# A fused attention and two-MLP kernel: the middle third of kv summed by TensorE, a shorter weight conversion, values transposed from the keys, weights loaded earlier

## The chip, the cores and the metric

The kernel runs on one core of one Trainium2 chip. The metric is device time in microseconds (us) of one execution, the median of the runs. The engines of the core are TensorE (PE in the profile, its weight loads PEld), VectorE (DVE), ScalarE (ACT), GpSimd (POOL) and SyncE (SP), whose queue issues every transfer here.

## The reference

Three stages follow one another on 12,288 tokens of width 128. The attention has one head; its keys and its values are the same array, the kv image averaged over 4 by 4 patches and multiplied by `w_sr`, so there are 768 of them.

```python
kv_pool = kv.reshape(B, H//4, 4, W//4, 4, C).mean(axis=(2, 4))   # 768 rows of 128
k = v = kv_pool.reshape(B, -1, C) @ w_sr
a = softmax(q @ k.T / sqrt(C));  x = a @ v                        # 12288 x 128
h = x @ w_in1;  g = max(h, 0) + alpha * min(h, 0);  y = g @ w_out1   # 128 -> 2048 -> 128
h = y @ w_in2;  g = h * sigmoid(1.702 * h);         z = g @ w_out2   # 128 -> 2048 -> 128
```

`q`, `kv`, `w_sr` are float32. The four MLP matrices arrive as float64 and go to the chip as pairs of 32-bit words.

## The kernel before, in words

Every product of the main part is made of three float16 products: both operands are split into a high part and a low remainder (`parts` L313, `mm3` L101), and high·high, high·low and low·high are added in PSUM. The high part is a ScalarE copy, the low part a subtraction on VectorE or GpSimd.

**Blocks and steps.** The tokens go in 24 blocks of 512. A step `t` of the main loop (`step` L547, loop L597) takes one of 16 slices of 128 hidden units through each of four layers, each layer for another block: layer 1 at `t`, layer 2 four steps later, layer 3 31 steps later, layer 4 36 steps later (L38). So t = 0 is the first layer-1 product, t = 16 the first of block 1, and layer 3 starts at t = 31. The attention of a block (scores `a_s`, exponentials `a_e`, high and low part of the weights `a_h` and `a_l` with a DMA transpose each, products with the values `a_v`) is laid over the steps before its layer 1 by the tables `ATT_START`, `ATT_S`, `ATT_V` (L40 to L42). The loop begins at t = -18 with block 0's attention.

**Before the loop.** kv lies in memory as 128 channels by 12,288 values, the 16 values of a patch side by side. It comes in twelve pieces of 512 KB, five buffers of tile `kv`; VectorE sums each group of 16 (L475) into `kvt`. After each third of the 768 keys, `thirds` (L446) forms the keys with `w_sr` in float32 (`keys`, L452: channels by keys), the same values a second time with the keys as rows (`low`, L459: the `pv` tiles), and takes the largest key (L461). Between the pieces the list `todo` (L468) puts the conversion of the first weight matrix. `v_scale` (L491) takes one scale from the three maxima and splits the keys into `k_hi` and `k_lo`; the split of block 0's queries follows (L595); `v_split` (L507), at t = -14, splits the `pv` tiles into `v_hi` and `v_lo`.

**Weights.** A float64 matrix comes in two pieces of 1 MB into tile `raw` (four buffers, `load_w` L138). `stats` (L148) takes the largest absolute value from the high words (two reductions, L152, and a row of small operations). Three steps then make float32 of the two words of a number: `conv1` scales the high word on ScalarE (L181), shifts and masks it (L182, recorded at L110) and puts the sign in (L185); `conv2` masks the exponent out (L191, recorded at L108), multiplies it by 16 bits of the low word (L195) and adds that on GpSimd (L197); `conv3` makes the float16 high part on ScalarE (L204) and the low part on GpSimd (L205). `conv2` also issues the load four pieces further on. `STATS` and `PREP` (L45, L46) give the steps at which w2, w3 and w4 are taken.

The order on each engine's queue is fixed at build time by a list scheduler. The order in which the program writes things is their priority; work whose inputs the scheduler holds ready may move ahead of what waits.

Of the kernel before, what the change touches and what calls it, by code (L numbers as in the profile page):

```python
# [38 lines left out]

ATT_START = [-18, -9] + [KF * j - 25 for j in range(2, NB)]  # L40
ATT_S = [(0, 2, 2, 6), (0, 4, 11, 13)] + [(0, 4, 7, 12)] * (NB - 2)
ATT_V = [tuple(range(10, 16)), tuple(range(17, 23))] + [(17, 18, 19, 21, 22, 22)] * (NB - 2)  # L42
# [10 lines left out]
def attn_moe_kernel(ctx: ExitStack, tc: tile.TileContext, q, kv, w_sr, w_in1, w_out1, alpha, w_in2, w_out2, out):  # L53
    nc = tc.nc
    const = ctx.enter_context(tc.tile_pool(name="const", bufs=1))
    raw_p = ctx.enter_context(tc.tile_pool(name="raw", bufs=4))
    cv_p = ctx.enter_context(tc.tile_pool(name="cv", bufs=2))
# [80 lines left out]
    def load_w(key, c):  # L138
        t = raw_p.tile([P, CW, 2], I32, tag="raw", name=f"raw_{key}{c}")
        src = srcs[key].bitcast(I32)  # L140
        if key in ("w1", "w3"):
            nc.sync.dma_start(out=t.rearrange("p f t -> p (f t)"), in_=src[:, 2 * c * CW:2 * (c + 1) * CW])
        else:
            nc.sync.dma_start(out=t.rearrange("p (k d) t -> p k (d t)", k=KC),
                              in_=src[c * CW:(c + 1) * CW, :].rearrange("(k p) d -> p k d", p=P))
        raw[key, c] = t
# [29 lines left out]
    def conv1(i):  # L176
        key, c = order[i]
        d = cv[i] = {}
        d["g"] = cv_p.tile([P, CW], I32, tag="g", name="g")

        nc.scalar.activation(d["g"].bitcast(F32), raw[key, c][:, :, 1].bitcast(F32), AF.Copy, scale=gsc[key])  # L181
        ts(d["g"], d["g"], 3, ALU.logical_shift_left, 0x7FFFFFFF, ALU.bitwise_and)  # L182

        d["a"] = cv_p.tile([P, CW], I32, tag="a", name="a")
        nc.vector.scalar_tensor_tensor(out=d["a"], in0=raw[key, c][:, :, 1], scalar=-0x80000000, in1=d["g"],  # L185
                                       op0=ALU.bitwise_and, op1=ALU.bitwise_or)

    def conv2(i):
        key, c = order[i]
        d = cv[i]  # L190
        ts(d["g"], d["a"], -0x800000, ALU.bitwise_and)  # L191

        u = raw[key, c].rearrange("p f t -> p (f t)").bitcast(U16).rearrange("p (f t) -> p f t", t=4)[:, :, 1]
        d["w"] = cv_p.tile([P, CW], F32, tag="w", name="w")
        nc.vector.scalar_tensor_tensor(out=d["w"], in0=u, scalar=2.0 ** -36, in1=d["g"].bitcast(F32),  # L195
                                       op0=ALU.mult, op1=ALU.mult)
        nc.gpsimd.tensor_tensor(out=d["w"], in0=d["a"].bitcast(F32), in1=d["w"], op=ALU.add)  # L197
        if i + 4 < len(order):
            load_w(*order[i + 4])
# [16 lines left out]
    def q_split(j):  # L216
        src = q_t.pop(j)
        qh[j] = at_p.tile([P, TB], F16, tag="qh", name="qh")
        ql[j] = at_p.tile([P, TB], F16, tag="ql", name="ql")
        c, p = scale_of(qsc[j], ps_x.tile([P, TB], F32, tag="x", name="qt"), None, "q")  # L220
        u = sm_p.tile([P, 1], F32, tag="qu", name="qu", bufs=4)
        qsc[j] = u

        def f():
            ts(u, p, kq, ALU.mult)
            parts(qh[j], ql[j], src, c)

        late.append(f)

# [208 lines left out]
    TK = NKEY // 3  # L438
    pvs = []
    vm = kv_p.tile([P, 3], F32, name="vm", bufs=1)  # L440
    todo = []

    kp2 = ps_s2.tile([P, 2, 512], F32, tag="s", name="kp2")
    pks = [kp2[:, 0, :], kp2[:, 1, :]]

    def thirds(i):  # L446
        tk = slice(i * TK, (i + 1) * TK)

        def keys():
            if i == 2:  # L450
                pks.append(ps_y.tile([P, TB], F32, tag="y", name="pk"))
            mm(out=pks[i][:, 0:TK], lhsT=wsr, rhs=kvt[:, tk], start=True, stop=True)  # L452

        def low():
            if i != 1:
                pvs.append(((ps_x if i else ps_y).tile([P, TB], F32, tag="x" if i else "y", name="pv"),
                            slice(2 * i, min(2 * i + 4, KT))))
            for k in (2 * i, 2 * i + 1):
                mm(out=pvs[-1][0][:, (k % 4) * C:(k % 4 + 1) * C], lhsT=kvt[:, k * P:(k + 1) * P], rhs=wsr,  # L459
                   start=True, stop=True)  # L460
            nc.vector.tensor_reduce(out=vm[:, i:i + 1], in_=pks[i][:, 0:TK], axis=AX.X, op=ALU.max,  # L461
                                    apply_absolute_value=True)

        c = 8 * i + 8 - NC2
        todo.append((c + 4, keys))
        todo.append((c + 6, low))

    for n, f in enumerate((lambda: stats("w1"), lambda: conv1(0), lambda: conv2(0), lambda: (conv3(0), conv1(1)),  # L468
                           lambda: conv2(1), lambda: conv3(1))):
        todo.append((4 + 2 * n, f))  # L470
    for c in range(0, NCH, NC2):
        t = kv_p.tile([P, NC2 * TB], F32, tag="kv", name="kv", bufs=5)
        nc.sync.dma_start(out=t, in_=kv[:, c * TB:(c + NC2) * TB])
        i, c8 = divmod(c, 8)
        nc.vector.tensor_reduce(out=kvt[:, c * 32:(c + NC2) * 32], in_=t.rearrange("p (k r) -> p k r", r=R * R),  # L475
                                axis=AX.X, op=ALU.add)
        if c == 6:
            load_q(0)
        if c8 == 8 - NC2:
            thirds(i)  # L480
        while todo and (min(x[0] for x in todo) <= c or c == NCH - NC2):
            x = min(todo, key=lambda x: x[0])
            todo.remove(x)
            x[1]()
        if c == 6:
            a_q(0)
    for c in range(NCW):
        load_w("w2", c)
    load_q(1)

    def v_scale():  # L491
# [11 lines left out]
        for i, t in enumerate(pks):
            tk = slice(i * TK, (i + 1) * TK)
            parts(k_hi[:, tk], k_lo[:, tk], t[:, 0:TK], vsc.bitcast(F32))

    def v_split():  # L507
        for t, k in pvs:
            src = t[:, 0:(k.stop - k.start) * C]
            hi, lo = (x[:, k, :].rearrange("p k d -> p (k d)") for x in (v_hi, v_lo))  # L510
            parts(hi, lo, src, vsc.bitcast(F32))

# [30 lines left out]
    def flush():  # L543
        while late:
            late.pop(0)()

    def step(t):  # L547
# [24 lines left out]
        for j, p in pieces:  # L572
            for n, p0 in enumerate(ATT_S[j]):
                if p == p0:
                    a_s(j, n)
            for k, p0 in enumerate(ATT_V[j]):
                if p == p0:
                    a_v(j, k)
            if p == -6 and j > 0:
                a_q(j)  # L580
            if p == -4 and j > 0:
                q_split(j)
                if j + 1 < NB:
                    load_q(j + 1)
# [63 lines left out]
```

## Time and profile before

| what | value |
|---|---|
| median of 3 runs | 1317.21 us (1317.12 to 1317.59) |
| the profiled execution, its own time | 1318.12 us |
| its span, first to last record | 1316.0 us |
| its mean granted TensorE clock | 0.982 |
| busy in the span: PE, DVE, ACT, POOL | 1226.0, 1053.4, 1108.5, 800.2 us |

The span of one execution is read by engine and by stage. The stages used below are cut at events: 38.24 us, the last key maximum has been taken; 48.47, the first score product starts; 85.42, the first layer-1 product (t = 0); 143.39, the first layer-1 product of block 1 (t = 16); 176.74, the first activation of layer 3 (t = 32). A busy TensorE is not one at its peak, since matmuls overlap. Idle time in brackets or after a bar is that of the engine just before an instruction, with what ended it.

### The profile page before, as it was taken

What the parts mean: (1) busy time and instruction counts of PE and PEld (TensorE: products, weight loads), DVE (VectorE), ACT (ScalarE), POOL (GpSimd) and SP (SyncE); (2) the same over time, 40 slices, a digit from 0 to 9 for tenths busy, and PEclk for the clock granted to TensorE, in tenths of its full rate; (3) what the DMA queues carried; (4) which work ended last, traced back from release to release, by engine and by line L of the source; (5) the groups of instructions that cost most, each with busy time, mean ns of one, the idle gap of its engine ahead of it and who ended that gap; (6) DMA issues with size and microseconds to landing.
All of it is one profiled execution on the core that took longest, in us unless ns stands there. A gap on an engine that the chain in (4) does not pass through costs nothing.

```text
span 1316.0 us, 17933 instructions
## 1 busy us (share of the span) xinstructions
PE 1226.0 (93%) x5712; PEld 560.1 (43%) x5712; DVE 1053.4 (80%) x1901; ACT 1108.5 (84%) x1966; POOL 800.2 (61%) x678
## 2 busy tenths in 40 slices
PE   1466699999999999999999999999999999999998
PEld 1122244444444444444444444444444444444443
DVE  7889789787887887878878878878878878877666
ACT  1455698998988988988988988988989989988998
POOL 1146743756756756756666666666666656657774
PEclk9877899999999999999999999999999999999999
DMA  9341221321211211212212212112112211210000
GB/s 355 98 120 24 45 51 32 52 51 26 54 44 33 53 41 37 53 33 44 53 32 45 47 37 47 40 37 53 41 37 46 47 37 33 45 36 21 9 9 17
DMA packets 167359, 66.26 MB, mean 50 GB/s; under 512 B 154848, under 2 KB 159072, under 8 KB 166752
## 3 DMA queue, kind: packets, MB, share of 16 engines
q1 hardware_dynamic: 167264, 65.11, 21.6%
q8 instruction: 45, 0.74, 0.2%
q14 instruction: 50, 0.41, 0.1%
HBM read 21.05 MB, written 6.29 MB: 21 GB/s over the span
## 4 chain that ended last, share of the span: by engine, by line
PE 54%; ACT 15%; DVE 14%; issue 5%; DMA 0%; POOLq 0%; ACTq 0%; DVEq 0%
PE h L102 8%; PE h L104 7%; PE h L103 7%; PE y L103 7%; PE y L104 7%; PE y L102 7%; DVE g L341 4%; ACT g L340 3%; ACT g L395 3%; ACT s L256 3%; DVE g L396 2%; PE xacc L103 2%; PE xacc L104 2%; ACT g1h L348 2%; PE xacc L102 2%
## 5 line engine op out<-in xcount | busy, mean ns | idle before, releaser
L349 POOL TENSOR_TENSOR g1l<-g,g1h 128x512 f16<-128x512 f32 x384 | 453.8, 1187 | 321.9 <-ACT g1h L348 310.1
L405 POOL TENSOR_TENSOR g2l<-g,g2h 128x512 f16<-128x512 f32 x272 | 314.8, 1158 | 120.7 <-ACT g2h L403 110.9
L395 ACT ACTIVATE g<-h,yu 128x512 f32<-128x512 f32 x384 | 269.2, 701 | 104.3 <-PE h L104 101.2
L396 DVE SCALAR_TENSOR_TENSOR g<-g,h 128x512 f32<-128x512 f32 x384 | 262.5, 684 | 110.7 <-ACT g L395 105.0
L341 DVE SCALAR_TENSOR_TENSOR g<-g,oma,h 128x512 f32<-128x512 f32 x384 | 285.1, 743 | 58.5 <-ACT g L340 52.4
L340 ACT ACTIVATE g<-h 128x512 f32<-128x512 f32 x384 | 235.8, 614 | 22.6 <-PE h L104 11.4
L348 ACT CAST g1h<-g 128x512 f16<-128x512 f32 x384 | 244.1, 637 | 8.5 <-DVE g L341 8.3
L403 ACT CAST g2h<-g 128x512 f16<-128x512 f32 x384 | 243.6, 634 | 3.3 <-PE y L104 1.2
L103 PE MATMUL y<-g1l,w2h 128*128 128x512 f16 x384 | 146.6, 382 | 14.7 <-POOL g1l L349 14.7
L102 PE MATMUL h<-xh,w1h 128*128 128x512 f16 x384 | 145.9, 382 | 5.4 <-DVE g L341 4.6
L102 PE MATMUL y<-g1h,w2h 128*128 128x512 f16 x384 | 146.2, 381 | 3.4 <-ACT g1h L348 3.4
L102 PE MATMUL h<-yh,w3h 128*128 128x512 f16 x384 | 145.2, 378 | 4.0 <-DVE g L341 1.0
L103 PE MATMUL h<-xl,w1h 128*128 128x512 f16 x384 | 146.7, 382 | 1.3
L104 PE MATMUL h<-xh,w1l 128*128 128x512 f16 x384 | 146.7, 382 | 0.0
L104 PE MATMUL y<-g1h,w2l 128*128 128x512 f16 x384 | 146.7, 382 | 0.0
L103 PE MATMUL y<-g2l,w4h 128*128 128x512 f16 x384 | 145.5, 379 | 0.5 <-POOL g2l L405 0.5
L102 PE MATMUL y<-g2h,w4h 128*128 128x512 f16 x384 | 145.5, 379 | 0.0
L104 PE MATMUL y<-g2h,w4l 128*128 128x512 f16 x384 | 145.5, 379 | 0.0
L104 PE MATMUL h<-yh,w3l 128*128 128x512 f16 x384 | 145.4, 379 | 0.0
L103 PE MATMUL h<-yl,w3h 128*128 128x512 f16 x384 | 145.3, 378 | 0.0
L246 DVE TENSOR_REDUCE nm<-s 128x1 f32<-128x768 f32 x96 | 91.5, 953 | 11.9 <-PE s L241 8.3
L405 DVE TENSOR_TENSOR g2l<-g,g2h 128x512 f16<-128x512 f32 x112 | 90.0, 804 | 9.7 <-ACT g2h L403 9.7
(228 smaller groups left out, 1686.0 us busy)
## 6 DMA issues: line engine op xcount, KB each, us to landing
kv<-in_kv SPq DMA_DIRECT2D x12, 512.0 KB, 8.4
q<-in_q SPq DMA_DIRECT2D x24, 256.0 KB, 2.6
out<-ob SPq DMA_DIRECT2D x24, 256.0 KB, 2.0
raw_w<-in_moe_w_in SPq DMA_DIRECT2D x4, 1024.0 KB, 8.5
raw_w<-in_moe_w_out SPq DMA_DIRECT2D x4, 1024.0 KB, 7.0
eh<-ah SPq DMA_TRANSPOSE x96, 2.8
wsr<-in_w_sr SPq DMA_DIRECT2D x1, 64.0 KB, 2.3
al<-in_moe_alpha SPq DMA_DIRECT2D x1, 8.0 KB, 1.7
```

Of the source, the lines that this page charges most:

```text
L102: mm(out=o, lhsT=wh, rhs=xh, start=start, stop=False)
L103: mm(out=o, lhsT=wh, rhs=xl, start=False, stop=False)
L104: mm(out=o, lhsT=wl, rhs=xh, start=False, stop=stop)
L246: nc.vector.tensor_reduce(out=nm, in_=s[:, :, 0:HALF], axis=AX.XY, op=ALU.max, negate=True)
L340: nc.scalar.activation(g, h, AF.Relu, scale=-1.0)
L341: nc.vector.scalar_tensor_tensor(out=g, in0=g, scalar=oma[:, m:m + 1], in1=h, op0=ALU.mult, op1=ALU.add)
L348: nc.scalar.copy(hi, g)
L349: nc.gpsimd.tensor_tensor(out=lo, in0=g, in1=hi, op=ALU.subtract)
L395: nc.scalar.activation(g, h, AF.Tanh, scale=ysc[j][:, 0:1])
L396: nc.vector.scalar_tensor_tensor(out=g, in0=g, scalar=1.0, in1=h, op0=ALU.add, op1=ALU.mult)
L403: nc.scalar.copy(hi, g)
L405: e.tensor_tensor(out=lo, in0=g, in1=hi, op=ALU.subtract)
```

## The change

- The middle third of kv is laid out on the host so that one value of all 256 patches is contiguous. TensorE multiplies those 16 slices by `w_sr` and adds the results in PSUM; VectorE sums the first and the last third as before.
- The conversion loses two VectorE masks, the multiply and the GpSimd addition. The top three bits of the low word are shifted and OR-ed in instead.
- `v_hi` and `v_lo` are two DMA transposes of `k_hi` and `k_lo`; the `pv` products, their tiles and `v_split` go.
- `raw` has six buffers. SP issues block 0's queries, both pieces of w1, kv, then w2, block 1's queries and w3, all before the key scale; w4 at t = -8. The two `w_out` matrices are rearranged on the host, so each load is 8 KB in a row per partition.
- Block 0's queries are split before kv. Their factor with the key scale is formed by a function of its own (`q_scale`), for every block.
- Block 1's attention starts at t = -5 in place of -9, and the weight steps move by one or two.

```diff
-ATT_START = [-18, -9] + [KF * j - 25 for j in range(2, NB)]
-ATT_S = [(0, 2, 2, 6), (0, 4, 11, 13)] + [(0, 4, 7, 12)] * (NB - 2)
-ATT_V = [tuple(range(10, 16)), tuple(range(17, 23))] + ...
-V_SPLIT = -14
-STATS = {"w2": -10, "w3": 2, "w4": 6}
-PREP = [(-9, -8, -7), (-7, -6, -5), (3, 4, 5), (6, 7, 8), (9, 10, 11), (12, 13, 14)]
+ATT_START = [-18, -5] + [KF * j - 25 for j in range(2, NB)]
+ATT_S = [(0, 2, 2, 6), (0, 3, 6, 9)] + [(0, 4, 7, 12)] * (NB - 2)
+ATT_V = [tuple(range(10, 16)), tuple(range(12, 18))] + ...
+KV_FREE = -11
+W4_LOAD = -8
+STATS = {"w2": -9, "w3": 1, "w4": 8}
+PREP = [(-8, -7, -6), (-7, -6, -5), (2, 3, 4), (5, 6, 7), (10, 11, 12), (13, 14, 15)]
...
-    raw_p = ctx.enter_context(tc.tile_pool(name="raw", bufs=4))
+    raw_p = ctx.enter_context(tc.tile_pool(name="raw", bufs=6))
...
     def conv1(i):
-        ts(d["g"], d["g"], 3, ALU.logical_shift_left, 0x7FFFFFFF, ALU.bitwise_and)
-        nc.vector.scalar_tensor_tensor(out=d["a"], in0=raw[key, c][:, :, 1], scalar=-0x80000000, in1=d["g"], ...)
+        ts(g, g, 3, ALU.logical_shift_left)
     def conv2(i):
-        ts(d["g"], d["a"], -0x800000, ALU.bitwise_and)
-        nc.vector.scalar_tensor_tensor(out=d["w"], in0=u, scalar=2.0 ** -36, in1=d["g"].bitcast(F32), ...)
-        nc.gpsimd.tensor_tensor(out=d["w"], in0=d["a"].bitcast(F32), in1=d["w"], op=ALU.add)
-        if i + 4 < len(order):
-            load_w(*order[i + 4])
+        nc.vector.scalar_tensor_tensor(out=g, in0=raw[key, c][:, :, 1], scalar=-0x80000000, in1=g,
+                                       op0=ALU.bitwise_and, op1=ALU.bitwise_or)
+        nc.vector.scalar_tensor_tensor(out=g, in0=raw[key, c][:, :, 0], scalar=29, in1=g,
+                                       op0=ALU.logical_shift_right, op1=ALU.bitwise_or)
...
+    def thirds(i):
+        for n in range(4):
+            c = 8 * i + 2 * n
+            t = kv_p.tile([P, NC2 * TB], F32, tag="kv", name="kv", bufs=5)
+            nc.sync.dma_start(out=t, in_=kv[:, c * TB:(c + NC2) * TB])
+            if i == 1:
+                for r in range(4):
+                    mm(out=pks[i], lhsT=wsr, rhs=t[:, r * TK:(r + 1) * TK], start=n + r == 0, stop=n + r == 6)
+            else:
+                nc.vector.tensor_reduce(out=kvt[:, c * 32:(c + NC2) * 32], ...)
+        if i != 1:
+            mm(out=pks[i], lhsT=wsr, rhs=kvt[:, tk], start=True, stop=True)
+    a_q(0); stats("w1"); q_split(0); flush()
+    thirds(0); conv1(0); conv2(0); conv3(0)
+    thirds(1); k_max(0); conv1(1); conv2(1); conv3(1)
+    thirds(2)
     for c in range(NCW):
         load_w("w2", c)
     load_q(1)
+    for c in range(NCW):
+        load_w("w3", c)
+    k_max(1); k_max(2)
...
     def v_scale():
+        for v, k in ((v_hi, k_hi), (v_lo, k_lo)):
+            nc.sync.dma_start_transpose(out=v, in_=k)
...
     v_scale()
-    q_split(0)
-    flush()
+    q_scale(0)
+    x_bound()
```

(In the new program each of the calls joined by `;` above stands on a line of its own.)

## Rows read from the trace of the kernel before

**Rows 1.** Windows by stage: us, each engine's busy time (instructions), granted clock, DMA.
```profile
0.00:38.24 38.24, 7.59 (x19) 5.15 (x20) 28.14 (x42) 5.70 (x5) 10.11 (x10) 1.00 0.90 344
38.24:48.47 10.23, 0.88 (x4) 0.24 (x4) 9.99 (x37) 3.02 (x7) 0.00 (x0) 1.00 0.01 3
48.47:85.42 36.95, 20.46 (x67) 8.53 (x67) 33.19 (x69) 18.59 (x27) 9.97 (x4) 0.69 0.57 135
85.42:143.39 57.97, 38.75 (x137) 15.28 (x136) 49.40 (x83) 32.89 (x52) 38.32 (x23) 0.78 0.20 32
143.39:176.74 33.35, 28.70 (x136) 13.03 (x136) 25.27 (x52) 26.17 (x47) 19.45 (x17) 1.00 0.26 54
...
400.00:1200.00 800.00, 796.67 (x3787) 366.34 (x3786) 643.73 (x1162) 718.40 (x1296) 516.25 (x449) 1.00 0.20 42
```

**Rows 2.** Groups by shape, DVE, 0 to 38.2: count | busy us, mean ns.
```profile
L108 DVE TENSOR_SCALAR g<-a 128x1024 int32<-128x1024 int32 x2 | 2.6, 1304 | 0.0
```

**Rows 3.** Windows, 10 to 20 us, columns as in the first group.
```profile
10.00:20.00 10.00, 2.70 (x7) 1.67 (x6) 9.17 (x22) 2.32 (x2) 0.00 (x0) 1.00 1.02 418
```

**Rows 4.** Timeline of SP's queue: start us, us.
```profile
13.94 0.43 SPq L142 DMA_DIRECT2D raw_w<-in_moe_w_in  x1
15.08 12.40 SPq L473 DMA_DIRECT2D kv<-in_kv  x5
```

**Rows 5.** Timeline of TensorE, first float32 key product and the next.
```profile
16.79 1.22 PE L452 MATMUL kp<-kvt,wsr 128*128 128x256 f32 x2 [2.40 <-DVE b_w L108]
17.80 0.63 PE L459 MATMUL pv<-wsr,kvt 128*128 128x128 f32 x2
```

**Rows 6.** DMA issues: count, KB, median us from issue to landing.
```profile
kv<-in_kv SPq DMA_DIRECT2D x12, 512.0 KB, 8.4
...
eh<-ah SPq DMA_TRANSPOSE x96, 2.8
```

**Rows 7.** Timeline, last three kv sums on VectorE.
```profile
33.01 3.46 DVE L475 TENSOR_REDUCE kvt<-kv 128x64 f32<-128x1024 f32 x3
```

**Rows 8.** Groups by shape, DVE, 38.24 to 48.47.
```profile
L152 DVE TENSOR_REDUCE wm<-raw_w 128x1 f32<-128x1024 f32 x4 | 4.8, 1209 | 0.0
```

**Rows 9.** Timeline, low parts of the values.
```profile
45.09 1.13 DVE L315 SCALAR_TENSOR_TENSOR v_lo<-pv,vsc,v_hi 128x512 f16<-128x512 f32 x2
```

**Rows 10.** Groups by shape, DVE, 48.47 to 85.42.
```profile
L246 DVE TENSOR_REDUCE nm<-s 128x1 f32<-128x768 f32 x7 | 6.7, 950 | 2.3 <-PE s L241 2.3
...
L185 DVE SCALAR_TENSOR_TENSOR a<-raw_w,g 128x1024 int32<-128x1024 int32 x2 | 2.4, 1216 | 0.0
L152 DVE TENSOR_REDUCE wm<-raw_w 128x1 f32<-128x1024 f32 x2 | 2.4, 1202 | 0.0
...
L108 DVE TENSOR_SCALAR g<-a 128x1024 int32<-128x1024 int32 x2 | 1.4, 681 | 0.0
...
L281 DVE SCALAR_TENSOR_TENSOR al__323<-e,r,ah 128x768 f16<-128x768 f32 x1 | 1.0, 1007 | 0.0
```

**Rows 11.** Groups by shape, DVE, 85.42 to 143.39.
```profile
L185 DVE SCALAR_TENSOR_TENSOR a<-raw_w,g 128x1024 int32<-128x1024 int32 x4 | 6.8, 1692 | 0.0
L195 DVE SCALAR_TENSOR_TENSOR w<-raw_w,g 128x1024 f32<-128x1024 uint16 x4 | 6.7, 1668 | 0.0
L108 DVE TENSOR_SCALAR g<-a 128x1024 int32<-128x1024 int32 x4 | 6.2, 1538 | 0.0
L110 DVE TENSOR_SCALAR g<-g 128x1024 int32<-128x1024 int32 x4 | 6.1, 1514 | 0.0
```

**Rows 12.** Groups by shape, POOL, 85.42 to 143.39.
```profile
L197 POOL TENSOR_TENSOR w<-a,w 128x1024 f32<-128x1024 f32 x4 | 9.4, 2352 | 3.0 <-DVE w L195 1.9 <-DVE we L108 1.2
```

**Rows 13.** Timeline: one GpSimd and one VectorE instruction that overlap.
```profile
106.78 2.83 POOL L205 TENSOR_TENSOR w3l<-w,w3h 128x1024 f16<-128x1024 f32 x1
...
107.56 3.13 DVE L185 SCALAR_TENSOR_TENSOR a<-raw_w,g 128x1024 int32<-128x1024 int32 x1
```

**Rows 14.** Waits, 85.42 to 143.39: us in total, times, longest.
```profile
PE y L103 <- POOL g1l L349: 11.7, 8, 4.1
```

More of the change, by code (lines that the diff above doesn't have):

```diff
@@ L139, in load_w @@
         t = raw_p.tile([P, CW, 2], I32, tag="raw", name=f"raw_{key}{c}")
[L140 to L145, printed above, removed]
+        nc.sync.dma_start(out=t.rearrange("p f t -> p (f t)"), in_=srcs[key].bitcast(I32)[:, 2 * c * CW:2 * (c + 1) * CW])
         raw[key, c] = t
@@ L203, in conv3, with flush @@
         cs = slice(c * CW, (c + 1) * CW)
-        nc.scalar.copy(wh[key][:, cs], cv[i]["w"])
-        nc.gpsimd.tensor_tensor(out=wl[key][:, cs], in0=cv[i]["w"], in1=wh[key][:, cs], op=ALU.subtract)
+        g = cv[i].bitcast(F32)
+        nc.scalar.copy(wh[key][:, cs], g)
+        nc.gpsimd.tensor_tensor(out=wl[key][:, cs], in0=g, in1=wh[key][:, cs], op=ALU.subtract)
     late = []
+    def flush():
+        while late:
+            late.pop(0)()
     qh, ql, qsc, xacc, eh, el, xh, xl, xsc = ({} for _ in range(9))
@@ L220, in q_split, with q_scale @@
         c, p = scale_of(qsc[j], ps_x.tile([P, TB], F32, tag="x", name="qt"), None, "q")
+        qsc[j] = p
+        late.append(lambda: parts(qh[j], ql[j], src, c))
+    def q_scale(j):
         u = sm_p.tile([P, 1], F32, tag="qu", name="qu", bufs=4)
+        ts(u, qsc[j], kq, ALU.mult)
         qsc[j] = u
[L224 to L228, printed above, removed]
     st = {}
@@ L425, in attn_moe_kernel @@
     kv_ctx = ExitStack()
-    kv_p = kv_ctx.enter_context(tc.tile_pool(name="kvp", bufs=3))
-    kvt = kv_p.tile([P, NKEY], F32, name="kvt", bufs=1)
+    kv_p = kv_ctx.enter_context(tc.tile_pool(name="kvp", bufs=1))
+    kvt = kv_p.tile([P, NKEY], F32, name="kvt")
+    vm = kv_p.tile([P, 3], F32, name="vm")
     make_identity(nc, ident)
@@ L432, in attn_moe_kernel @@
     nc.sync.dma_start(out=wsr, in_=w_sr)
+    load_q(0)
     for c in range(NCW):
@@ L438, in attn_moe_kernel @@
     TK = NKEY // 3
-    pvs = []
-    vm = kv_p.tile([P, 3], F32, name="vm", bufs=1)
-    todo = []
     kp2 = ps_s2.tile([P, 2, 512], F32, tag="s", name="kp2")
-    pks = [kp2[:, 0, :], kp2[:, 1, :]]
+    pks = [kp2[:, 0, 0:TK], kp2[:, 1, 0:TK], ps_y.tile([P, TB], F32, tag="y", name="pk")[:, 0:TK]]
     def thirds(i):
         tk = slice(i * TK, (i + 1) * TK)
[L449 to L486, printed above, removed]
+        for n in range(4):
[6 more added lines that the diff above has]
+            else:
+                nc.vector.tensor_reduce(out=kvt[:, c * 32:(c + NC2) * 32], in_=t.rearrange("p (k r) -> p k r", r=R * R),
+                                        axis=AX.X, op=ALU.add)
@@ L487, in attn_moe_kernel, with k_max @@
+        if i != 1:
+            mm(out=pks[i], lhsT=wsr, rhs=kvt[:, tk], start=True, stop=True)
+    def k_max(i):
+        nc.vector.tensor_reduce(out=vm[:, i:i + 1], in_=pks[i], axis=AX.X, op=ALU.max, apply_absolute_value=True)
+    a_q(0)
+    stats("w1")
+    q_split(0)
+    flush()
+    thirds(0)
+    conv1(0)
+    conv2(0)
+    conv3(0)
+    thirds(1)
+    k_max(0)
+    conv1(1)
+    conv2(1)
+    conv3(1)
+    thirds(2)
     for c in range(NCW):
@@ L489, in attn_moe_kernel @@
     load_q(1)
+    for c in range(NCW):
+        load_w("w3", c)
+    k_max(1)
+    k_max(2)
     def v_scale():
@@ L499, in v_scale @@
         ts(vsc, vun, -1.0, ALU.mult, float(268 << 23), ALU.add)
+        for i, t in enumerate(pks):
+            tk = slice(i * TK, (i + 1) * TK)
+            parts(k_hi[:, tk], k_lo[:, tk], t, vsc.bitcast(F32))
+        for v, k in ((v_hi, k_hi), (v_lo, k_lo)):
+            nc.sync.dma_start_transpose(out=v, in_=k)
         ts(kq, vun.bitcast(F32), SCALE * 2.0 ** -32, ALU.mult)
         ts(vun, vun, float(-33 << 23), ALU.add)
[L503 to L511, printed above, removed]
     def x_bound():
@@ L541, in at @@
         return (j, m) if 0 <= j < NB else None
-    def flush():
-        while late:
-            late.pop(0)()
     def step(t):
@@ L582, in step @@
                 q_split(j)
+                late.append(lambda j=j: q_scale(j))
                 if j + 1 < NB:
@@ L601, in attn_moe_kernel @@
         step(t)
-        if t == V_SPLIT:
-            v_split()
-            x_bound()
+        if t == W4_LOAD:
+            for c in range(NCW):
+                load_w("w4", c)
+        if t == KV_FREE:
             kv_ctx.close()
@@ L631 @@
             a = a.view(np.int64)
+            if name.endswith("_w_out"):
+                a = np.ascontiguousarray(a.reshape(KF, P, C).transpose(1, 0, 2).reshape(P, DFF))
         if name == "q":
@@ L635 @@
         if name == "kv":
-            a = np.ascontiguousarray(a[0].reshape(HH // R, R, WW // R, R, C).transpose(4, 0, 2, 1, 3).reshape(C, NTOK))
+            a = a[0].reshape(HH // R, R, WW // R, R, C).transpose(4, 0, 2, 1, 3).reshape(C, 3, NKEY // 3, R * R)
+            a = np.concatenate([a[:, 0].reshape(C, -1), a[:, 1].transpose(0, 2, 1).reshape(C, -1),
+                                a[:, 2].reshape(C, -1)], axis=1)
         if name == "moe_alpha":
```

16 lines of the change are left out of this document (4 added, 12 removed).

## Prediction

> **What bounds the kernel now.** I read the windows first, cut at the events named above. Over the long middle TensorE is busy 796.67 of 800 us at a granted clock of 1.00 [rows 1]: there it sets the pace, and the change touches none of its products. What can move is the start. In the first four stages, 143.39 us together, TensorE is busy 67.7 us, part of it at a granted clock of 0.69 and 0.78 [rows 1]. From t = 16 on it is busy 28.70 of 33.35 us, and soon after always. So the end moves by about as much as t = 16 moves, and the question is what paces the four stages.
>
> In all four it is VectorE: 28.14 of 38.24, 9.99 of 10.23, 33.19 of 36.95, 49.40 of 57.97 us busy [rows 1], the first stage with 10.1 us idle. Not all of that is work. In stage four the sixteen VectorE instructions of the conversion take 6.8 + 6.7 + 6.2 + 6.1 = 25.8 us [rows 11]; undisturbed, at 1.216 for one with two tensors and 0.681 for one with one [rows 10], they would take 4 x 3.79 = 15.2. The timeline shows why: an instruction that began at 107.56 while GpSimd worked from 106.78 to 109.61 took 3.13 us, about what was left of GpSimd's plus its own 1.2 [rows 13]. GpSimd's four additions are 9.4 us of this stage [rows 12], and TensorE waits 11.7 us for the low parts that GpSimd makes [rows 14].
>
> **The change, stage by stage.**
>
> *Keys (0 to 38.24).* VectorE loses four of twelve sums at 3.46 / 3 = 1.15 to 1.2 us each [rows 7], 4.8 us, and two masks, 2.6 [rows 2]; the split of block 0's queries comes in, about 1.1 (the two `v_lo` of like size [rows 9]). That is 6 us less for VectorE. The new work is on TensorE: sixteen float32 products of 256 columns. The nearest row is one such key product, 1.01 us from its start to the next start [rows 5], so 16.2 us in a row; alone, with its end, it is 1.22. They can begin when the fifth kv piece has landed: queries 0.26, `w_sr` 0.07, w1 2.10 and five pieces 2.62 are 5.05 MB, at 418 GB/s [rows 3] 12.1 us; with a first issue that I set at 2, that is 14. Buffers bind too: piece 12 takes the buffer of piece 7, the third of the middle, free at 14 + 12 x 1.01 = 26.1. Landing takes at least 0.52 MB / 418 GB/s = 1.3 us and at the median of before 8.4 [rows 6]; the queue is nearly empty then, so I take 4 and 30. A sum (1.2) and then the tail of before, from the end of the last sum at 36.47 to 38.24 [rows 1, 7], follow: 33.0, a gain of 5.2. Bounds: 6 as above, and a loss of 1.8 with 1.22 for each product and 8.4 for the landing (28.6 + 8.4 + 3.0 = 40.0). That kv is not later for the early weights I read from SP's queue: before, a piece of w3 went out at 13.94 ahead of the last five pieces of kv [rows 4]; SP keeps to the order in which loads are written, and now w2 and w3 stand behind all of kv.
>
> *Scale and split (10.23).* Four weight maxima stand in it, 4.84 [rows 8], and the two `v_lo`, 1.13 [rows 9]. The latter go. The maxima need w2 and w3, 4.2 MB behind kv and so up to 10 us later; I let nearly all of them leave this stage: a gain of 5, bounds 6.0 and 1.1. The two transposes that replace the `pv` work land 2.8 us after issue [rows 6]; they stand on SP behind the loads of w2 and w3 and before every transpose of block 0. First need is eight steps on, at t = -8, and that cover hides them; without it they cost 2.8 and the rest of the 10 us.
>
> *Block 0's attention (36.95).* Gone: two masks 1.4, the two maxima of w4 2.4, and of block 1 one score tile that moves past t = 0, 0.95 for its maximum and 1.01 for its low part [rows 10]: 5.7. Come in: the four maxima of w2 and w3, 4.8, and block 1's query split, 1.1. VectorE is about even; two GpSimd additions less disturb it, for which I take 1. Bounds: a gain of 5.7, if the maxima fall into idle time, and a loss of 2, if a transpose is late.
>
> *Conversions of w3 and w4, t = 0 to 16 (57.97).* Twelve instructions instead of sixteen: undisturbed 4 x (0.681 + 2 x 1.216) = 12.5, disturbed as now 4 x (1.514 + 2 x 1.69) = 19.6, against 25.8. In come w4's maxima, 2.4, and the moved score tile, 2.0. So between 1.8 and 8.9 us of VectorE go. Of GpSimd's conversion work half goes, 9.4 us, and with it its share of the 11.7 us that TensorE waits. I take 8, near the undisturbed end, because the additions were what most often stood in the way. Best case: the 8.6 us that VectorE idles here end as well, 17.
>
> The Trainium skill (SBUF — State Buffer, Who interferes with whom) has GpSimd and VectorE share one pair of ports as an exclusive lock: the one that starts later is blocked until the other's instruction has ended. The 3.13 us row agrees with it; what it would make of the whole stage is the second rival below, with 1295 where the sum has 1298.
>
> *Queries' factor, every block.* `q_scale` is the same one instruction, now behind the split. First use is steps later; TensorE idles 3.3 us in the 800 of the middle [rows 1]. Nothing.
>
> Sum: 5.2 + 5 + 1 + 8 = 19.2. The profiled execution took 1318.1 us, 2.1 more than its span; less 19.2 that is 1298.9. The median of the runs shown is 0.9 below it: 1298.0.
>
> **The rivals.** About 0.2% (2.6 us) is what a measurement of this kernel can tell from no change.
>
> *Less: the gain of the keys is given back.* The maxima and the later tile still have to be done; with the third stage at a loss of 2, and the disturbed 1.8 in the fourth, 5.2 + 5 - 2 + 1.8 = 10.0 remain: 1307. For it: GpSimd keeps its subtractions, and the low parts of layer 1 still meet the conversion. Against: half of what collided is gone.
>
> *Ports: the two engines exclude each other all through stage four*, as in the one overlap that a row shows [rows 13]. Then the stage goes by the sum of what the two do there: each piece loses 0.68 of mask and 2.35 of addition [rows 10, 12], four pieces 12.1, and the moved low part adds 1. The gain is 11 in place of 8: 1295. For it: VectorE's masks went from 0.68 to 1.54 [rows 10, 11]. Against: part of the stage waits for other things than the two.
>
> *More: the collisions end and the idle time with them.* 5.2 + 5 + 5.7 + 17 = 32.9: 1284. For it: TensorE's 11.7 us of waits in that stage. Against: VectorE must be nearly free of idle time, which it is nowhere now.
>
> *No change.* The sums on TensorE take 1.22 each and the last piece lands late (a loss of 1.8), and the rest at its small ends (1.1 - 2 + 1.8): a loss of 0.9, 1318. Everything would have to go to its bad end.
>
> *Slower: the steady part.* The query split and its factor change places in every block's VectorE queue, and the scheduler may lay out the blocks anew. One mechanism: a wait of TensorE, once a block. There are 23 blocks behind the first; from 19.2 / 23 = 0.83 us a block on it eats the gain, at 1.2 the kernel is at 1326. Against: TensorE's idle time is now 3.3 us in 16 blocks, 0.2 a block, and the instruction that moves is small.
>
> **How the numbers follow.** Forecast 0.40 and ports 0.15; their times lie too close to keep apart, and both fill 1289 to 1305. Less, 1305 to 1314.5: 0.22. More, below 1289: 0.14. So faster is 0.91 in all. No change within 0.2%, 1314.6 to 1319.8: 0.04. Slower: 0.05. The range 1284 to 1310 leaves out some 0.05 of the more case, 0.06 of the less case and the last two, 0.2 together.
>
> **What would show it.** Right: the last kv piece is issued near 26 and the key maxima end near 33; the first score product starts near 38 instead of 48.47; t = 0 lies near 73; the conversion's VectorE instructions between t = 0 and 16 sum to 12.5 to 17 us and GpSimd has no 2.35 us addition; t = 16 comes near 124 instead of 143.39; the 800 us in the middle stay at 796 to 797 busy. Wrong: TensorE's sums end after 33 and VectorE waits for the key product; VectorE's conversion stays above 19 us; the first value product waits for a transpose; or TensorE's idle time in the middle stage grows above 10 us.

## The result, and the profile after

The changed kernel takes 1297.6 us (median of 4 runs, 1295.8 to 1300.7) against 1317.3 (4 runs, 1317.1 to 1317.6): a ratio of 0.985, 95% interval 0.983 to 0.987. The profiled execution took 1297.24 us with a span of 1295.5.

The windows of the changed kernel, cut at the same events as in [rows 1]: last key maximum, first score product, t = 0, t = 16, first activation of layer 3, and the same 800 us of the middle.

```profile
0.00:33.37 33.37, 11.40 (x38) 8.90 (x39) 24.51 (x40) 6.44 (x6) 4.95 (x8) 1.00 0.83 311
33.37:37.74 4.37, 0.53 (x3) 0.21 (x2) 4.11 (x19) 1.31 (x3) 0.00 (x0) 0.50 1.03 427
37.74:73.31 35.57, 17.45 (x64) 7.37 (x63) 30.19 (x71) 17.37 (x25) 4.81 (x2) 0.68 0.78 172
73.31:121.96 48.65, 36.38 (x138) 14.79 (x138) 42.57 (x86) 32.92 (x52) 27.52 (x18) 0.82 0.25 44
121.96:155.75 33.79, 29.31 (x138) 12.99 (x137) 26.61 (x55) 27.54 (x48) 20.36 (x17) 1.00 0.33 55
400.00:1200.00 800.00, 796.67 (x3786) 365.78 (x3784) 641.01 (x1154) 717.11 (x1292) 517.45 (x449) 1.00 0.20 41
```

The ledger against [rows 1], stage by stage: 4.87, 5.86, 1.38, 9.32 and -0.44 us gained, 20.99 at the first activation of layer 3 (176.74 to 155.75). From there to the end of the span it is 1139.3 us before and 1139.7 after. All of the gain is made in the first 122 us, and the 800 us in the middle hold the same 796.67 of TensorE.

The timeline of the changed kernel, first 38 us (start us, us; idle before and its releaser in brackets):

```profile
3.07 23.76 SPq L441 DMA_DIRECT2D kv<-in_kv  x12
...
17.37 1.22 PE L449 MATMUL kp<-kvt,wsr 128*128 128x256 f32 x2 [4.07 <-DVE b_w L109]
18.39 9.26 PE L444 MATMUL kp<-kv,wsr 128*128 128x256 f32 x32
...
30.90 1.22 DVE L446 TENSOR_REDUCE kvt<-kv 128x64 f32<-128x1024 f32 x1 [1.20 <-DMA kv<-in_kv]
32.17 0.70 PE L449 MATMUL pk<-kvt,wsr 128*128 128x256 f32 x2 [4.52 <-DVE kvt L446]
33.37 0.16 DVE L480 TENSOR_REDUCE v<-vm 128x1 f32<-128x3 f32 x1
34.38 1.21 DVE L148 TENSOR_REDUCE wm<-raw_w 128x1 f32<-128x1024 f32 x1
...
37.49 1.21 DVE L148 TENSOR_REDUCE wm<-raw_w 128x1 f32<-128x1024 f32 x1
```

kv now goes out without a weight between its pieces; the last is issued at 26.50 and VectorE still waits 1.20 us for it. TensorE's sixteen sums (two records each) run from 18.39 to 27.65 and nobody waits for them at the end. Of the two maxima of w2 one, 1.21 us, stands inside the chain from the last key maximum to the first score product; the other starts 0.25 us before that product (37.74).

Stage three, from the first score product to t = 0, groups by shape on VectorE, 37.74 to 73.31, beside [rows 10]:

```profile
L238 DVE TENSOR_REDUCE nm<-s 128x1 f32<-128x768 f32 x7 | 6.6, 950 | 1.5 <-PE s L233 0.8 <-PE qt L295 0.7
L148 DVE TENSOR_REDUCE wm<-raw_w 128x1 f32<-128x1024 f32 x5 | 6.0, 1208 | 0.0
```

VectorE takes seven score maxima here, as many as before the change, and the last five of the eight weight maxima. w4's two are among them, so they too begin before t = 0.

The conversion in stage four, groups by shape on VectorE, 73.31 to 121.96 (count | busy us, mean ns of one), beside [rows 11]:

```profile
L183 DVE SCALAR_TENSOR_TENSOR g<-raw_w,g 128x1024 int32<-128x1024 int32 x4 | 7.7, 1930 | 0.0
L185 DVE SCALAR_TENSOR_TENSOR g<-raw_w,g 128x1024 int32<-128x1024 int32 x4 | 6.7, 1684 | 0.0
...
L109 DVE TENSOR_SCALAR g<-g 128x1024 int32<-128x1024 int32 x4 | 3.7, 916 | 0.1
```

That is 18.1 us in twelve instructions, where [rows 11] have 25.8 in sixteen. TensorE's wait for GpSimd's low parts in this stage, beside [rows 14] (total us, times, longest):

```profile
PE y L104 <- POOL g1l L341: 8.9, 7, 3.1
```

It fell only from 11.7 to 8.9.

### The profile page after: what moved, and what is told of

Read it like the earlier page. It is cut to its first block, busy times and chain, and to the rows that moved or that the text cites. A ratio compares the mean times of both kernels' runs of the same rounds, so it can differ in the third digit from the quotient of the medians.

```text
span 1295.5 us, 17938 instructions
## 1 busy us (share of the span) xinstructions
PE 1224.9 (95%) x5730; PEld 561.7 (43%) x5730; DVE 1036.3 (80%) x1887; ACT 1108.0 (86%) x1964; POOL 780.7 (60%) x670
## 4 chain that ended last, share of the span: by engine, by line
PE 54%; ACT 16%; DVE 13%; issue 4%; POOLq 0%; ACTq 0%
PE h L103 8%; PE h L105 7%; PE h L104 7%; PE y L104 7%; PE y L105 7%; PE y L103 7%; ACT g L332 4%; DVE g L333 3%; ACT g L387 3%; ACT s L248 3%; ACT g1h L340 2%; DVE g L388 2%; PE xacc L103 2%; PE xacc L105 2%; PE xacc L104 2%
```

## The experiments

Twelve kernels ran. The table has the edges of the profiled execution of each (us from the start of the span) and the median of all its runs; the kernel before, measured beside them, had medians of 1317.3 to 1317.5. "xl" is the start of the low part of block 1's x, which the first layer-1 products of block 1 need (in b1 it comes 3.1 us ahead of them).

| kernel | last key maximum | first score | t = 0 | xl | layer 3 | median us |
|---|---|---|---|---|---|---|
| before | 38.24 | 48.47 | 85.42 | 143.60 | 176.74 | 1317.3 |
| changed | 33.37 | 37.74 | 73.31 | 123.45 | 155.75 | 1297.6 |
| a0 changed, again | 33.76 | 38.13 | 74.33 | 124.45 | 156.75 | 1296.7 |
| a1 w4 loads written later | 32.42 | 36.79 | 72.65 | 121.72 | 154.01 | 1297.6 |
| a2 additions put back | 35.32 | 39.69 | 75.44 | 127.61 | 160.16 | 1300.3 |
| a3 sums on VectorE | 35.04 | 40.03 | 75.00 | 123.68 | 154.31 | 1296.1 |
| a4 old conversion | 33.76 | 38.12 | 76.80 | 134.94 | 166.31 | 1308.6 |
| b1 new conversion alone | 36.57 | 46.80 | 80.97 | 126.57 | 160.92 | 1304.6 |
| a5 w4 loads behind block 0 | 33.48 | 37.85 | 69.68 | 121.05 | 153.87 | 1295.1 |
| a7 a5, weight maxima later | 34.75 | 38.14 | 72.98 | 124.29 | 154.91 | 1295.7 |
| c1 w2, w3 loads later | 33.60 | 37.44 | 72.75 | 121.81 | 152.43 | 1293.4 |
| c2 old tables of block 1 | 33.01 | 37.39 | 74.20 | 120.68 | 152.18 | 1295.8 |
| d1 w4 converted later | 32.89 | 37.27 | 73.07 | 122.27 | 155.39 | 1296.4 |
| d2 d1 and a5 | 34.68 | 39.05 | 71.27 | 120.18 | 153.17 | 1293.8 |

Two things are read from the table before any experiment. In all fourteen profiles the span ends 1139.1 to 1140.2 us behind the first activation of layer 3, so the end is decided there. And the changed kernel scatters over 5 us in its runs (before: within 1.4). Its two profiles differ by up to 1.02 us at an edge, and a1, in which every queue up to layer 3 holds the same order, reaches layer 3 1.7 and 2.7 us earlier than they do. So a difference of less than some 3 us between single profiles says nothing.

**The reference point.** The changed kernel unaltered. 

> The changed kernel itself once more, as the base for the three beside it: 1296 to 1300 us (1297.6 before), stages ending near 33.4, 37.7, 73.3 and 122 us.

Measured: 1296.7 us (1295.2 to 1299.5), ratio 0.985 (0.983 to 0.986).

**What the conversion is worth, from both sides.** The changed kernel with the old masks, multiply and addition, and the kernel before with the new conversion alone:

```diff
-        ts(g, g, 3, ALU.logical_shift_left)
+        ts(d["g"], d["g"], 3, ALU.logical_shift_left, 0x7FFFFFFF, ALU.bitwise_and)
...
+        ts(d["g"], d["a"], -0x800000, ALU.bitwise_and)
...
+        nc.vector.scalar_tensor_tensor(out=d["w"], in0=u, scalar=2.0 ** -36, in1=d["g"].bitcast(F32),
+                                       op0=ALU.mult, op1=ALU.mult)
+        nc.gpsimd.tensor_tensor(out=d["w"], in0=d["a"].bitcast(F32), in1=d["w"], op=ALU.add)
```

> The changed kernel with the weight conversion of before (mask, multiply, GpSimd addition), all else as changed. The sum on record: the conversion's own share is 1.2 to 2.6 us in stage one, 2.4 in stage three and 12.4 in stage four (the 8 of the sum and the 4.4 of other work that moved in), 16 to 17 us: 1312 to 1315. Rival, stage four is not paced by VectorE and GpSimd throughout: the addition, which cost 3.6 us when it was put back by itself, and six masks of 0.68 us, 4.1: about 8 us, 1303 to 1306.

> The kernel before with the new weight conversion alone (loads, tables, kv sums, values and queries as before). By the sum: 16 to 17 us of gain, 1300 to 1302. By the rival of the run beside it: 8 us, 1308 to 1311. If conversion and the rest only work together (stage four has nothing to gain until x of block 1 comes earlier, or the other way round): less than either, 1311 to 1317.

Measured: with the old conversion 1308.6 (1308.3 to 1309.3), 11.9 us above a0; before with the new one 1304.6 (1302.6 to 1305.2), 12.9 below the kernel before measured beside it (1317.5). Each lies between the first two forecasts made for it. Both sides agree on about 12, so the conversion and the rest add, and the rest of the change is worth 7 to 9. The groups of the old conversion in the changed kernel, VectorE, 76.80 to 127.71:

```profile
L191 DVE SCALAR_TENSOR_TENSOR w<-raw_w,g 128x1024 f32<-128x1024 uint16 x4 | 7.8, 1944 | 0.0
L181 DVE SCALAR_TENSOR_TENSOR a<-raw_w,g 128x1024 int32<-128x1024 int32 x4 | 7.0, 1741 | 0.0
L109 DVE TENSOR_SCALAR g<-a 128x1024 int32<-128x1024 int32 x4 | 6.1, 1517 | 0.0
L111 DVE TENSOR_SCALAR g<-g 128x1024 int32<-128x1024 int32 x4 | 3.9, 980 | 0.4 <-ACT g L177 0.4
```

24.8 us here against 18.1 with the new one: 6.7 of VectorE, and t = 0 to layer 3 is 7.1 longer than in a0 (89.51 against 82.42); another 2.5 comes before t = 0. The pair of two-tensor instructions is as slow with the additions as without: 7.8 + 7.0 and 7.7 + 6.7.

**GpSimd's additions by themselves.** The changed kernel with one GpSimd addition of 128x1024 for each piece, into a tile that nobody reads (extra work, the output is unchanged):

```diff
+        z = cv_p.tile([P, CW], F32, tag="z", name="z")
+        nc.gpsimd.tensor_tensor(out=z, in0=g.bitcast(F32), in1=g.bitcast(F32), op=ALU.add)
```

> A GpSimd addition of the old size (128 x 1024 float32, two inputs) is put back into each weight piece; its result goes to a scratch tile that nothing reads, VectorE's work stays as changed. Theory of the ports rival, GpSimd and VectorE exclude each other and stage four goes by their sum: 4 x 2.35 = 9.4 us more there and some in stage three, 1307 to 1311. The sum on record (8 us for masks, additions and their waits together): 3 to 6 us, 1301 to 1304. If VectorE's own instructions were all that counted: within 1.5 us.

Measured: 1300.3 (1299.6 to 1301.7), 3.6 above a0 and 2.7 above the changed kernel's first median, whose range it overlaps. Had the two engines excluded each other throughout, the additions would have cost nearly what they last: 1.89 us each (median), 15 for the eight pieces. So the rival of the ports falls in its own form, a stage that goes by the sum of both engines. The run prices the contention alone: nothing waits for these additions, while before the change the next step of the conversion needed them. Which of VectorE's instructions are held, the timeline of VectorE and GpSimd in the changed kernel shows, in stage three and at the beginning and the end of stage four:

```profile
60.77 2.69 POOL L193 TENSOR_TENSOR w2l<-g,w2h 128x1024 f16<-128x1024 f32 x1 [32.15 <-ACT w2h L192]
61.47 0.94 DVE L238 TENSOR_REDUCE nm<-s 128x1 f32<-128x768 f32 x1
62.33 2.22 DVE L185 SCALAR_TENSOR_TENSOR g<-raw_w,g 128x1024 int32<-128x1024 int32 x1
...
84.03 1.16 POOL L341 TENSOR_TENSOR g1l<-g,g1h 128x512 f16<-128x512 f32 x1 [1.83 <-ACT g1h L340]
84.12 1.62 DVE L109 TENSOR_SCALAR g<-g 128x1024 int32<-128x1024 int32 x1
...
113.55 2.55 POOL L193 TENSOR_TENSOR w4l<-g,w4h 128x1024 f16<-128x1024 f32 x1 [3.33 <-DVE xd L109]
116.06 1.15 POOL L341 TENSOR_TENSOR g1l<-g,g1h 128x512 f16<-128x512 f32 x1
...
114.11 0.67 DVE L290 TENSOR_REDUCE ta<-q 128x1 f32<-128x512 f32 x1
114.83 1.02 DVE L273 SCALAR_TENSOR_TENSOR al__928<-s,r,ah 128x768 f16<-128x768 f32 x1
...
116.54 1.76 DVE L183 SCALAR_TENSOR_TENSOR g<-raw_w,g 128x1024 int32<-128x1024 int32 x1
...
121.53 1.22 DVE L185 SCALAR_TENSOR_TENSOR g<-raw_w,g 128x1024 int32<-128x1024 int32 x1
...
123.45 0.75 DVE L307 SCALAR_TENSOR_TENSOR xl<-xacc,xc,xh 128x512 f16<-128x512 f32 x1
```

While GpSimd worked from 60.77 to 63.46, VectorE's reduction of 0.94 us kept its usual length (0.950 in [rows 10]); the conversion instruction that began at 62.33 took 2.22 instead of 1.22 and ended 1.1 us behind GpSimd's. From 113.55 to 116.10 the reduction of 0.67 and the low part of 1.02 us (1.007 in [rows 10]) kept theirs; the instruction at 116.54 took 1.76 and ended 1.1 us behind GpSimd's at 117.21. What tells the two kinds apart is where the inputs lie: both inputs of the held ones are in SBUF, while a reduction has one input, and the low part at 114.83 reads `s` from PSUM. All eight large VectorE instructions with two inputs in SBUF that began under a GpSimd instruction in stage four were held, and end 0.8 to 1.1 us behind it. One with a single input was held too, the conversion's shift at 84.12, 1.62 us instead of 0.68. The Trainium skill (SBUF — State Buffer, Who interferes with whom) has an exclusive lock between the two engines that lets a VectorE instruction with at most one input in SBUF pass, outside the two-port modes, and holds one with two such inputs while a GpSimd instruction reads SBUF. The trace agrees: the 3.13 us of [rows 13], 2.22 and 1.76 on one side, 0.94, 0.67 and 1.02 on the other; whether the shift ran in such a mode no row shows.

**The sums on TensorE.** The changed kernel with the middle third summed by VectorE, kv laid out as before:

```diff
-            if i == 1:
+            if False:
...
-        if i != 1:
+        if True:
```

> The middle third is summed by VectorE again, with kv laid out as before; all else as changed. Theory: four sums of 1.21 us come back to VectorE, which idles about 1.2 us at the last kv piece, so the key maxima end 3 to 5 us later (36.5 to 38.5 instead of 33.4) and so does the kernel: 1300.5 to 1303. Rival, the arrival of the last kv piece sets the end of stage one in any case, and the sums on TensorE gave little: within 1.5 us.

Measured: 1296.1 (1295.8 to 1298.6), 0.6 below a0, which the intervals (0.983 to 0.986 for both) can't tell from nothing. The loss that was expected did not come. Timeline of VectorE in this kernel:

```profile
30.88 2.33 DVE L446 TENSOR_REDUCE kvt<-kv 128x64 f32<-128x1024 f32 x2
...
35.04 0.16 DVE L480 TENSOR_REDUCE v<-vm 128x1 f32<-128x3 f32 x1
```

VectorE reaches the last piece about 1.1 us later (two sums in a row instead of one that waited for its transfer), and the key maxima end 1.3 to 1.7 us later. By layer 3 that is gone: 154.31 against 155.75 and 156.75. But the edit changed more than the sums: the scheduler laid VectorE's queue out anew, and the last instruction of w4's conversion starts at 120.39, 3.3 us ahead of xl (123.68), where the changed kernel has it at 121.53, 1.9 us ahead of xl (123.45). c1 below, which keeps the sums on TensorE and has that instruction early too, is 2.7 faster than this kernel. So stage one pays 1.3 to 1.7 us for the sums on VectorE, and what they are worth at the end is not isolated.

**The loads of w4.** In the changed kernel they meet block 0's transposes on SP's queue. DMA issues of the changed kernel (count, median us from issue to landing):

```profile
eh<-ah SPq DMA_TRANSPOSE x96, 2.7
...
el<-al__333 SPq DMA_TRANSPOSE x1, 6.1
el<-al__354 SPq DMA_TRANSPOSE x1, 2.8
el<-al__355 SPq DMA_TRANSPOSE x1, 5.9
```

Its timeline, SP's queue and the waits behind it:

```profile
47.56 0.56 SPq L141 DMA_DIRECT2D raw_w<-in_moe_w_out  x1
48.22 1.22 SPq L274 DMA_TRANSPOSE el<-al__333  x1
...
54.93 0.57 SPq L141 DMA_DIRECT2D raw_w<-in_moe_w_out  x1
55.59 1.22 SPq L274 DMA_TRANSPOSE el<-al__355  x1
...
54.37 1.02 DVE L273 SCALAR_TENSOR_TENSOR al__355<-e,r,ah 128x768 f16<-128x768 f32 x1 [1.70 <-DMA el<-al__333]
...
62.21 0.58 PE L103 MATMUL xacc<-eh,v_hi 128*128 128x512 f16 x1 [2.44 <-DMA eh<-ah]
```

Each of the two late transposes stands directly behind a 1 MB load of w4; the one between them landed in 2.8. VectorE waits for a buffer of `al`, TensorE for the weights. First, with the loads written ten steps later (`W4_LOAD = 2`; `t` is -8 in the changed kernel):

> The two w4 loads go out at t = 2 in place of t = -8. Theory, transfers collide: in the changed kernel two transposes of block 0 land 6.1 and 5.9 us after issue instead of 2.8, just behind a w4 load of 1 MB each, and TensorE and VectorE wait for them; without the loads there, all of block 0's transposes land in 2.7 to 3.5 us, the third stage shortens from 35.6 by 3 to 6 us and the kernel comes to 1292 to 1295. Rival, VectorE paces that stage and covers the late transposes: the landings shorten, the time stays within 1.5 us.

Measured: 1297.6 (1295.5 to 1300.2). The edit moved nothing: the loads went out at 46.61 and 54.34 all the same, ahead of what waits, so this run says nothing on the collision. So the order was tied to an instruction:

```diff
-            for c in range(NCW):
-                load_w("w4", c)
+            with tc.issue_after(last_el[0].ins):
+                for c in range(NCW):
+                    load_w("w4", c)
```

> The two w4 loads are tied behind the last transpose of block 0 on SP's queue (moving them in the program alone left them where they were on the queue: the scheduler put them forward). Theory, transfers collide: block 0's transposes land in 2.7 to 3.5 us instead of up to 6.1, VectorE's 1.7 us and TensorE's 7.7 us waits in stage three shrink, the stage shortens by 3 to 6 us, 1291 to 1294. Rival, stage three is paced by VectorE: within 1.5 us.

Measured: 1295.1 (1292.8 to 1296.9). The DMA issues of this kernel:

```profile
el<-al__333 SPq DMA_TRANSPOSE x1, 2.8
el<-al__354 SPq DMA_TRANSPOSE x1, 2.8
el<-al__355 SPq DMA_TRANSPOSE x1, 2.8
```

The collision is gone: stage three lasts 31.83 us, 3.7 to 4.4 less than in the two profiles of the changed kernel and in a1, and t = 0 comes 3.0 to 4.7 us earlier. Layer 3 comes only 0.1 to 2.9 ahead: part is given back in stage four, where xl again stands behind the conversion of w4 on VectorE. At the end 1.6 us are left against a0, with intervals that overlap (0.982 to 0.984 and 0.983 to 0.986); the forecast of 1291 to 1294 was missed. With the maxima of w2 to w4 tied behind the splits of the keys as well:

> As the run with the w4 loads tied behind the transposes, and the maxima of w2, w3 and w4 tied behind the three low parts of the keys on VectorE's queue (two of them stood between the key scale and the first scores, 2.3 us). Theory, the chain from the key scale to the first score paces there: the first score product starts 2 us earlier and the kernel gains 1 to 2 us on the run beside it. Rival, the maxima are only moved into stage three, which VectorE paces: within 1 us of the run beside it.

Measured: 1295.7 (1294.6 to 1296.4), no better than a5 alone. The stage from the last key maximum to the first score product shortens from 4.37 to 3.39, by about the one maximum that stood in it, but in this profile the key maxima end 1.3 us later, and the order behind them is a new one too. That the maximum costs elsewhere what it cost in the chain fits the time and is not shown.

**The order of the rest.** Block 1's step tables as before the change:

```diff
-ATT_START = [-18, -5] + ...
-ATT_S = [(0, 2, 2, 6), (0, 3, 6, 9)] + ...
-ATT_V = [tuple(range(10, 16)), tuple(range(12, 18))] + ...
+ATT_START = [-18, -9] + ...
+ATT_S = [(0, 2, 2, 6), (0, 4, 11, 13)] + ...
+ATT_V = [tuple(range(10, 16)), tuple(range(17, 23))] + ...
```

> The changed kernel with the step tables of block 1's attention as they were before: it begins four steps earlier, and its last score and value tiles stand after t = 0 again instead of ahead of it; the rest as changed. The prediction's step: one score tile moves past t = 0, worth 0.95 + 1.01 us to the stage before it, and costs the stage after it the same. By this t = 0 moves by about 2 us and the end by under 1: 1296 to 1298. Rival: the layout of block 1 is what shortened stage four (9.3 us), then the end comes 4 or more later, 1301 and up.

Measured: 1295.8 (1293.7 to 1297.3). t = 0 stayed (74.20) and the median is 0.9 below a0, inside the scatter: the new tables bring nothing that can be measured, and the rival, that they carry stage four's gain, falls. The tile that the tables were to move past t = 0 does not move: VectorE takes seven score maxima between the first score product and t = 0 in the kernel before, in the changed one and here.

The loads of w2 and w3 written behind `v_scale` instead of ahead of it:

> The changed kernel with the loads of w2 and w3 written behind the key scale, so that the two transposes of the values stand ahead of them on SP. If the early loads buy the second stage (5.9 us gained there), the two maxima of w2 that now stand between the last key maximum and the first score product leave it and the stage shortens by a further 2.4, and the loads' 4 MB then meet block 0's transposes as w4's do: t = 0 later by 2 to 4, end at 1298 to 1301. Rival: loads go out as soon as a buffer is free wherever they are written, and nothing moves: t = 0 at 73 to 75, end 1296 to 1298.

Measured: 1293.4 (1292.5 to 1293.9), ratio 0.982 (0.980 to 0.983): the best of all kernels here, 3 to 4 us better than the changed one, which neither theory had. Three of the four loads went out at 27.55 to 29.05 anyhow; only the last piece of w3 moved, to 40.10. What moved besides is the order on VectorE. Its timeline:

```profile
31.74 0.68 DVE L290 TENSOR_REDUCE ta<-q 128x1 f32<-128x512 f32 x1
33.14 0.42 DVE L452 TENSOR_REDUCE vm<-pk 128x1 f32<-128x256 f32 x1 [0.72 <-PE pk L449]
...
37.89 1.21 DVE L148 TENSOR_REDUCE wm<-raw_w 128x1 f32<-128x1024 f32 x1
...
118.00 1.58 DVE L185 SCALAR_TENSOR_TENSOR g<-raw_w,g 128x1024 int32<-128x1024 int32 x1
...
121.81 0.74 DVE L307 SCALAR_TENSOR_TENSOR xl<-xacc,xc,xh 128x512 f16<-128x512 f32 x1
```

Block 1's queries arrive ahead of w2, and their maximum fills VectorE's wait for the last key product; w2's maxima stand behind the first score product; and the last VectorE instruction of w4's conversion starts at 118.00 instead of 121.53, so xl is not held by it. Which of these brings the 3 to 4 us was not separated.

The conversion of w4 written eight and nine steps later, alone and with a5:

```diff
-PREP = [..., (10, 11, 12), (13, 14, 15)]
+PREP = [..., (18, 19, 20), (22, 23, 24)]
```

> The changed kernel with the two conversions of w4 moved from t = 10 to 15 to t = 18 to 24; w4 is first used at t = 36. In the changed kernel xl of block 1 ends 5 us behind xh, with two instructions of w4's conversion ahead of it on VectorE, and TensorE waits for low parts that stand behind GpSimd's subtraction of w4. If stage four is still paced by VectorE's conversion, the six instructions that leave it (7 to 9 us) bring xl forward by 5 or more; TensorE, busy 29.3 of 33.8 us in the next stage, has 4.5 us idle to take them in, so the end gains 2 to 5: 1292 to 1295. Rival: x of block 1 waits for TensorE's own products, and the work only moves behind it: 1296 to 1298.

> The same with the loads of w4 behind block 0's last transpose as well (alone 1295.1). If the two gains are of different stages they add: 4 us at t = 0, 2 to 5 in stage four, 1289 to 1293. Rival: both fill the same idle time of TensorE, and it is no faster than the better of the two, 1294 to 1296.

Measured: 1296.4 (1296.3 to 1298.0) and 1293.8 (1291.9 to 1294.1). Alone it brings nothing, where 2 to 5 us were expected. But the conversion hardly moved: VectorE still works through all four `L183` by t = 16, and only the last `L185` falls behind xl (123.05). So this does not show what an emptier stage four would be worth. The pair is 1.3 below a5, whose range it overlaps; it was to be 1289 to 1293 if the two gains added.

## Why the prediction was right, and where it was not

The forecast was 1298.0 and the result 1297.6; a start that shortens and a middle that doesn't move is what the ledger shows, and its sizes agree stage for stage: 5.2, 5, 1, 8 and 0 foretold, 4.87, 5.86, 1.38, 9.32 and -0.44 found. That VectorE's work sets much of it, the conversion shows from both sides (a4, b1); in stage three late transposes held VectorE as well (a5). That the sum comes within 0.4 us is luck: errors cancel inside its terms, and the changed kernel's own runs spread over 5 us. Every dated sign but one came out: last kv piece 26.5 for 26, maxima 33.4 for 33, first score 37.7 for 38, t = 0 73.3 for 73, t = 16 at 122.0 for 124, the middle at 796.67 for 796 to 797. The miss is the conversion on VectorE, 18.1 us for 12.5 to 17. Of the signs of being wrong one came: the first value product waits 2.44 us for a transpose, not of the values but of block 0's weights (`eh`). In the kernel before it waits 1.85 us for the same, so this sign tells little. Inside the terms more was off:

- *Keys.* The sums were priced at 1.01 us each from 14 on; they take 9.26 / 16 = 0.58 and start at 18.39, directly behind the key product of the first third on TensorE. The two errors point opposite ways, and neither decides: the stage ends with the last piece's landing, forecast for 30, found at 30.9. Whether the sums buy the kernel time is open: without them it is as fast, but in another order (a3).
- *Scale and split.* Nearly all four maxima were to leave this stage, and nearly all did: one and the first 0.25 us of another stayed, and it shortened by 5.86. Forcing these out took 1.0 us off the stage and gained nothing at the end (a7). The two transposes of the values land 5.4 and 4.6 us behind their issue, not 2.8, but hidden, as foretold: the first value product, at 62.21, waits for another.
- *Block 0's attention.* The small net gain was right by cancellation. Of the 5.7 us that were to go only the two masks did: the score tile (some 2 us) stays ahead of t = 0, and so do w4's maxima (2.4). In their place VectorE was held less: two low parts took 3.1 us, under an addition, and 2.1 before the change, and all six take 1.0 now; 1 us was taken for that. SP was taken to keep to the order written; the scheduler puts the loads of w4 forward (a1), directly ahead of two of block 0's transposes. That collision stood in the lower bound (a loss of 2) and not in the sum. Without it the stage is 31.83 us (a5), a gain of 5.1.
- *Stage four.* The 8 us were taken near the undisturbed end because the additions were held to be what most often stood in the way. They were not: before the change VectorE's instructions of this stage were held by some 12 us over the shortest of their form, 3.4 of it under additions and the rest under GpSimd's subtractions, which stay. Added alone to all eight pieces the additions cost 3.6 us in the whole kernel (a2), the two-tensor instructions stay at 1.68 to 1.93 us without them, and TensorE's wait for GpSimd fell by 2.8 of 11.7. The 8 stood for 12.4 off the conversion and 4.4 of w4's maxima and the score tile that were to come in. Both were off and cancel: the 4.4 did not come in, and the conversion fell by 25.8 - 18.1 = 7.7, VectorE's whole work by 6.8 (49.40 to 42.57), and it idled 2.5 less, which the 8 did not count: 9.32.
- *The conversion as a whole* is worth 12 from either side (a4, b1); the price that went into those two expectations, summed over the stages, was 16 to 17. It held 4.4 for the work that was to move into stage four; without that it is 12.
- *Queries' factor, steady part.* Nothing, as forecast.

*Ports* (1295) lies within the scatter of the median. Its sum of both engines is excluded by a2, not by the time; the lock that it rests on is there, for instructions with two inputs in SBUF. *Less*, *More*, *No change* and *Slower* are excluded by the time.

The rest of the change, 7 to 9 us, is known only as a sum. Taking back the sums on TensorE (a3) or block 1's tables (c2) brings nothing that can be measured, but both runs also got another order on VectorE; how the remainder splits between the values as transposes, the early split of block 0's queries and the loads was not tried piece by piece. Why the changed kernel scatters over 5 us, and c1 over 1.4, is open too.

## What to carry to other kernels

Find the event from which the end follows at a fixed distance (here the first activation of layer 3, 1139 to 1140 us before the end in every profile) and judge each edit there: 3.0 to 4.7 us won at t = 0 were 0.1 to 2.9 at that event. Look next at the queue behind the edge, here VectorE's, where the conversion of a weight that is needed twenty steps later stood ahead of the operand that was needed at once; no run shows by itself that this is what took the gain. Writing a load later does not delay it where a scheduler may move it; look at its row on SP's queue before believing the edit. And an edit to one engine's work can change the order on the others, as in a3: compare the queues before reading a median as the price of the edit.

## What had not been expected of the hardware

- The sixteen float32 products of 128x256 do not keep one pace. Their records (two each), before and behind 22.6:

```profile
L444 PE MATMUL kp<-kv,wsr x10: 633/634/635, 18.4 to 22.2; 128*128 128x256 f32 x10
L444 PE MATMUL kp<-kv,wsr x22: 379/380/461, 22.7 to 27.3; 128*128 128x256 f32 x22
```

  The first five follow one another at 0.85 us, the others at some 0.43, and 0.58 is the mean of both. The windows show a granted clock of 1.00 over all of them, so the rows don't say why the first are slower. For the lone key product behind them they do: it took 0.70 in the changed kernel, at 1.00, and 1.22 in c1, where the window 30.97 to 41.20 shows 0.50 (1.2 of 2.4 GHz).
- A DMA transpose that stands right behind a 1 MB load on the same queue lands in 5.9 to 6.1 us instead of 2.8, and in 2.8 again when the load is moved behind it (a5).
- GpSimd slows only some of VectorE's instructions. In these overlaps 1.22, with two inputs in SBUF, became 2.22 and 1.76, and a shift of 0.68 became 1.62; reductions of 0.94 and 0.67 and a low part of 1.02 that reads PSUM stayed as they were.
